# Expert 0 of a routed layer: one list in two passes with the same weights, in place of two lists

## The chip, the cores and the metric

The kernel runs on one core of one Trainium2 chip. A core has five engines, each with an instruction stream of its own that it works through in order: TensorE (PE: matrix products, with weight loading PEld beside them), VectorE (DVE), ScalarE (ACT), GpSimd (POOL) and SyncE (SP), which here only issues transfers. Transfers run on 16 DMA engines. The metric is the device time of one execution in microseconds. The kernel before takes 766.38 us, the median of three runs (764.54, 766.38 and 768.68).

## The reference

Three layers, in float32. Attention with 8 heads of 64 over two sequences of 768 tokens, with a window of 128 and 4 sink tokens, gives x of 1536 x 512. A dense layer follows: h = x w_in, g = h - tanh(h), x = g w_out, with 2048 hidden units. The last layer is routed over 8 experts with 1024 hidden units each:

```
logits = x @ w_gate
noisy  = logits + log1p(exp(x @ w_noise)) * noise
top2   = the two largest of noisy, per token;  top2_w = softmax over the two
for e in range(8):
    for k in range(2):
        mask = top2[:, k] == e
        out[mask] += top2_w[mask, k, None] * (relu(x[mask] @ w1[e]) @ w2[e])
```

So each token goes through two of the experts, and which ones is known only when its row of the dense layer's output is there.

## The kernel before

**Split products.** Products are made in fp32r, TensorE's reduced float32. To keep the accuracy, both operands are split in two parts of that type, `hi` and `lo`: ScalarE casts `hi` (L231 for weights, L967 for rows), VectorE subtracts to get `lo` (L232, L969). Each product then is three: hi hi, lo hi, hi lo.

**Order of the work.** Tokens are 12 blocks of 128; two blocks are a chunk, and there are six chunks. The first 96 units (`N1`) are attention and the dense layer. The last two chunks are the late ones: their dense units come last. After a chunk's dense output its route is computed (`route`, a generator whose steps are called between the units of other work): logits, exp and log, the two largest, the token's position in the lists of its experts. GpSimd then scatters the token's row, with its weights and target row, into two lists in DRAM (`xs`).

**The routed layer.** A list is gathered from DRAM to SBUF as `xr` by four transfers that SP issues (`b_gather`, L909), turned by four VectorE transposes into `xf` (L949) and split into `xg`. `b_tab` fetches the table of weights and target rows, and `settle` (L936 to L939) makes the scale from it. Expert e then has eight units of 128 hidden columns, two per pair d of weights. A unit is `b_l1` (12 products into `h`, L984), `b_chain` (ScalarE relu L994, VectorE L995, which together give `hh`) and `b_l2` (12 products into the four accumulators `yacc`, L1008). At an expert's end `b_evac` copies the accumulators to `yt` (L1022), two by ScalarE and two by VectorE; during the next expert's first four units `b_out` turns them back (L1050), scales them and adds what was gathered of the output before (`prev`, by `b_prev`), and GpSimd stores the rows (L1036).

**Weights.** A pair's weights (1 MB) are loaded into `rawi<d>` by `load_d` (L187), in two buffers, and split into `wi<d>` and `wo<d>`, four buffers of each. A load is issued when the split two pairs earlier has freed its buffer; `emit` works on these splits step by step. Expert 0 has pairs 8 to 11, expert 1 has 12 to 15, and so on.

**Expert 0 in two lists.** While expert 0 runs, the late chunks are still being routed. Its list has 296 places and only rows of the early chunks. The late chunks' rows for expert 0 go to a ninth list of 160 places, which runs after expert 7 with weights loaded once more, in plain fp32 without a split (`c_rows`, `c_l1` L1066, `c_l2` L1078). All other lists have 424 places. Expert 1 begins when the late rows are scattered and gathered; the last route runs between expert 0's first units. Rows beyond a list's places are done by `beyond`, which is not entered with these inputs.

**What sets the order.** From unit N1 - 1 to N1 + 9 every engine's order is that of the code (`in_order`). Outside of that a scheduler places each engine's instructions by its own estimates, and each engine then takes them in that fixed order: one that waits holds up all behind it.

Of the kernel before, what the change touches and what calls it, by code (L numbers as in the profile page):

```python
# [16 lines left out]
P = 128  # L17
# [3 lines left out]
SLOTS_A = 296  # L21
SLOTS_B = 160
FAR = 1 << 20
EARLY_D = 12
# [47 lines left out]
def kernel(ctx: ExitStack, tc: tile.TileContext, qkv, vsink, w64, wm, wgn, noise, out,  # L72
# [14 lines left out]
    WB = SLOTS_B  # L87
# [4 lines left out]
    OT = (max(NT - W, LATE * CT - WA, NT - LATE * CT - WB) + P - 1) // P  # L92
    SEC = NT + P
    ROWS = (E + 1) * SEC
# [6 lines left out]
    N = N1 + E * NU2  # L101
# [71 lines left out]
    def load_d(kind, d, q=nc.sync):  # L173
        if kind == "c" and d >= 2:
            t = gp2.tile([P, 2048], F32, tag="wi", name=f"raw{kind}{d}", bufs=2)
        elif d != EARLY_D:
            t = wp.tile([P, 2048], F32, tag="raw", name=f"raw{kind}{d}", bufs=2)
        if d < 8 and kind != "c":
            q.dma_start(t.bitcast(I32), w64[d * 2 + (kind == "o")].bitcast(I32))
            raw[kind, d] = t  # L180
        elif kind == "c":
            q.dma_start(t, wm[d])
            raw["c", d] = t
        else:
            if d == EARLY_D:
                t = yp.tile([P, 4, 512], F32, tag="y", name=f"raw{kind}{d}", bufs=1).rearrange("p a n -> p (a n)")
# [492 lines left out]
    def route(c0, c1):  # L679
# [7 lines left out]
        tr = {}  # L687

# [44 lines left out]
        pos, ev, zz = [sm[:, i:i + 2] for i in range(2, 8, 2)]  # L733
# [36 lines left out]
        if c0 == LATE:  # L770
            V.tensor_copy(macc[:, T1], macc[:, T0])
            V.memset(macc[:, T1, 0:1], 0.0)
# [14 lines left out]
        if end:  # L787
            V.tensor_scalar(zz, ev, 0.0, float(E), op0=ALU.is_equal, op1=ALU.mult)
            V.tensor_add(ev, ev, zz)
# [4 lines left out]
        V.tensor_scalar(rs, dd, 1.0, 1e-9, op0=ALU.add, op1=ALU.add)  # L794
        V.reciprocal(rs, rs)
        for c in range(c0, c1):
            x, ms = x2s[c], slice((c - c0) * CB, (c - c0 + 1) * CB)
            xi = x.bitcast(I32)
            V.tensor_copy(x[:, :, 516], ev[:, 0, ms])
            V.tensor_copy(xi[:, :, 517], sl[:, 0, ms])  # L800
            V.tensor_copy(x[:, :, 514], rs[:, ms])
            V.tensor_mul(x[:, :, 515], dd[:, ms], rs[:, ms])
# [22 lines left out]
    def overflow_tiles():  # L825

        cnt = cst.tile([P, E + 1], F32, name="cnt")
        caps = cst.tile([P, E + 1], F32, name="caps")
        over = cst.tile([P, E + 1, OT], F32, name="over")
        full = cst.tile([P, E + 2], F32, name="full")  # L830
        nt = cst.tile([P, E + 2], I32, name="nt")
        nc.gpsimd.memset(caps, float(W))
        nc.gpsimd.memset(caps[:, 0:1], float(WA))
        nc.gpsimd.memset(caps[:, E:], float(WB))
        nc.vector.tensor_copy(cnt[:, 0:1], macc[:, LATE * CB, 0:1])
        nc.vector.tensor_copy(cnt[:, 1:E], macc[:, NBLK + 1, 1:])
# [18 lines left out]
    def width(v):  # L855
        return WA if v == 0 else WB if v == E else W

    def tiles(v):
        w = width(v)
        return [(m, o, min(P, w - o)) for m, o in enumerate(range(0, w, P))]  # L860
# [3 lines left out]
    def clear(v):  # L864
# [3 lines left out]
        if v <= E:  # L868
            n = (width(v) + P - 1) // P
# [5 lines left out]
        else:  # L875
            o = (v - E - 1) * NT // 3
# [20 lines left out]
    def b_gather(v):  # L897
        w = width(v)

        xr[v] = []  # L900
        ins = []
        for h, (g0, g1) in enumerate(parts(v)):
            if v:
                r = yp.tile([P, WP // 32, 4, 32], F32, tag="xr", name=f"xr{v}", bufs=1)
            else:
                r = wp.tile([P, 8, 4, 32], F32, tag="cacz"[2 * h:2 * h + 2], name=f"xr{v}_{h}", bufs=1)
            src = xs[v * SEC + 32 * g0:v * SEC + 32 * g1, :512].rearrange("(g t) (q c) -> q t g c", t=32, q=4)
            for q in range(4):
                ins.append(nc.sync.dma_start(r[32 * q:32 * q + 32, :g1 - g0].rearrange("t g k j -> t g (k j)"), src[q]))  # L909
            xr[v].append(r)  # L910
        behind(v, ins, scat)
        if v:
            b_tab(v)

    def behind(v, ins, scatters):

        for i in ins:
            for j in scatters:
                if v or j not in late:
                    wait_for(i, j)  # L920
                else:
                    tc.declare_no_dep(i.ins, j.ins, reason="different rows")
# [515 lines left out]
```

## Time and profile before

| | us |
|---|---|
| median of three runs | 766.38 |
| the profiled run | 767.55 |
| its span | 765.2 |
| TensorE busy in it | 722.1 |
| VectorE busy in it | 473.8 |
| ScalarE busy in it | 356.2 |
| GpSimd busy in it | 185.5 |

The span goes from the first instruction to the last; the profiled run's time is 2.35 us longer. Busy time tells which engine can set the time over all; where it does, and what it waits for, stands in the views by place, which are shown below as rows. A row of a timeline is a run of like instructions: start, length, engine and line, operation, output from input, tile and shape, count, and in brackets the idle time just before with what ended it. Lengths of rows overlap, because products are pipelined: the time of a group is read from its start to the next one's.

### The profile page before, as it was taken

Reading aid. Unit: us, or ns where it says so; the run is one execution under the profiler, and the core shown is the slowest. Engines: PE = TensorE matmul, PEld = TensorE weight load, DVE = VectorE, ACT = ScalarE, POOL = GpSimd, SP = SyncE. Lnnn points to the kernel's source line nnn. Section 1 sums busy time; section 2 is a strip of 40 time slices with the busy share of each in tenths; the row PEclk is TensorE's granted clock in tenths of the full one; section 3 lists DMA queues with packets and bytes.
Section 4 is the critical chain, followed back from the end, with each engine's and each line's share of the span. In section 5 each row is a group of like instructions: output and inputs, shape, how many; then the busy total and the mean of one; then the engine's idle time right before and its main releaser. Section 6 shows DMA issues by size and latency. Waiting matters only on the chain. (4 is left out here: it accounts for less than half of the span.)

```text
span 765.2 us, 12079 instructions
## 1 busy us (share of the span) xinstructions
PE 722.1 (94%) x4346; PEld 652.2 (85%) x4346; DVE 473.8 (62%) x1203; ACT 356.2 (47%) x785; POOL 185.5 (24%) x217
## 2 busy tenths in 40 slices
PE   6888889999999999999999979999999999999991
PEld 3575768888999999988888979999999999999991
DVE  5897658877877486437468666676656474543221
ACT  4877658775644344235446534444343434332110
POOL 5435436531000000000352221313131313132321
PEclk9999989999999999999999989999999999999997
DMA  8988851001432032000235387856657444444411
GB/s 297 247 244 232 213 200 49 24 1 56 166 110 93 18 116 105 1 1 1 84 132 193 125 219 217 238 158 193 190 184 184 165 156 154 151 144 162 155 73 35
DMA packets 64453, 104.96 MB, mean 137 GB/s; under 512 B 19661, under 2 KB 48973, under 8 KB 57728
## 3 DMA queue, kind: packets, MB, share of 16 engines
q1 hardware_dynamic: 57648, 83.35, 36.4%
q0 software_dynamic: 6592, 19.70, 7.6%
q10 hardware_dynamic: 144, 1.05, 0.3%
q8 instruction: 36, 0.59, 0.3%
q14 instruction: 33, 0.27, 0.1%
HBM read 79.12 MB, written 25.68 MB: 137 GB/s over the span
## 5 line engine op out<-in xcount | busy, mean ns | idle before, releaser
L984 PE MATMUL h<-xg,wi 128*128 128x424 f32 (+1 forms) x768 | 158.4, 356 | 4.2 <-ACT xg L967 4.2
L606 PE MATMUL h<-xT,wi 128*128 128x256 f32 x1152 | 157.6, 283 | 1.2 <-DVE th L616 1.2
L606 PEld LDWEIGHTS h<-xT,wi 128*128 128x128 f32 x1152 | 150.4, 189 | 8.2 <-DVE th L616 1.6
L1008 PE MATMUL y<-hh,wo 128*128 128x424 f32 (+1 forms) x768 | 152.1, 348 | 0.2 <-DVE yt L1022 0.2
L638 PE MATMUL acc<-wo,g 128*128 128x512 f32 x576 | 151.6, 397 | 0.0
L984 PEld LDWEIGHTS h<-xg,wi 128*128 128x128 f32 x768 | 139.7, 191 | 8.6 <-ACT xg L967 5.2
L1008 PEld LDWEIGHTS y<-hh,wo 128*128 128x128 f32 x768 | 139.5, 188 | 3.5 <-DVE yt L1022 0.8
L638 PEld LDWEIGHTS acc<-wo,g 128*128 128x128 f32 x576 | 101.9, 190 | 16.3
L994 ACT ACTIVATE hh<-h 128x424 fp32r<-128x424 f32 (+1 forms) x64 | 32.6, 511 | 150.7 <-PE h L984 148.1
L1036 POOL DMA_INDIRECT out<-y,tab x33 | 41.4, 1255 | 191.2 <-DVE y L1035 190.9
L805 POOL DMA_INDIRECT xs<-x,sl x24 | 27.1, 1130 | 236.5 <-PE acc L638 200.9
L995 DVE SCALAR_TENSOR_TENSOR hh<-h,hh 128x424 fp32r<-128x424 f32 (+1 forms) x64 | 37.1, 579 | 75.2 <-ACT hh L994 74.9
L406 POOL TENSOR_TENSOR e<-e,nm 128x528 f32<-128x528 f32 (+1 forms) x48 | 50.6, 1054 | 89.1 <-DVE nm L404 48.9
L619 ACT CAST g<-th 128x256 fp32r<-128x256 f32 x96 | 38.8, 405 | 57.0 <-PE acc L638 40.3
L614 ACT ACTIVATE th<-h 128x256 f32<-128x256 f32 x96 | 36.6, 381 | 59.6 <-PE h L606 57.7
L616 DVE TENSOR_TENSOR th<-h,th 128x256 f32<-128x256 f32 x96 | 40.3, 420 | 38.3 <-ACT th L614 37.9
L395 ACT ACTIVATE e<-e,nm 128x264 f32<-128x264 f32 (+1 forms) x96 | 47.1, 492 | 31.6 <-DVE nm L382 30.8
L621 DVE TENSOR_TENSOR g<-th,g 128x256 fp32r<-128x256 f32 x96 | 41.7, 435 | 23.2 <-ACT g L619 22.5
L486 PE MATMUL xb<-pT,v 128*128 128x256 f32 x220 | 49.0, 351 | 5.3 <-DVE xT L501 5.0
L232 DVE TENSOR_TENSOR wi<-rawi,wi 128x1024 fp32r<-128x1024 f32 x32 | 39.0, 1222 | 20.5 <-ACT wi L231 20.5
L486 PEld LDWEIGHTS xb<-pT,v 128*128 128x128 f32 x220 | 33.3, 196 | 15.6 <-issue 6.2
L889 POOL DMA_INDIRECT prev<-out,tab x33 | 35.7, 1082 | 43.2 <-DMA out<-y,tab 31.3
(170 smaller groups left out, 886.8 us busy)
## 6 DMA issues: line engine op xcount, KB each, us to landing
rawi<-wm SPq DMA_DIRECT2D x31, 1024.0 KB, 5.2
rawi<-w SPq DMA_DIRECT2D x8, 1024.0 KB, 4.8
rawo<-w SPq DMA_DIRECT2D x8, 1024.0 KB, 4.8
xs<-zero SPq DMA_DIRECT2D x7, 1040.0 KB, 7.3
xr<-xs SPq DMA_DIRECT2D x28, 224.0 KB, 6.4
qr<-qkv SPq DMA_DIRECT2D x23, 256.0 KB, 3.1
rawc<-wm SPq DMA_DIRECT2D x4, 1024.0 KB, 5.3
out<-zero SPq DMA_DIRECT2D x3, 1024.0 KB, 7.6
```

The source lines that it names most:

```text
L232: nc.vector.tensor_sub(t[:, 1], r, t[:, 0].bitcast(F32))
L395: nc.scalar.activation(e[:, h], e[:, h], AF.Exp, bias=nm[:, h, 0:1], scale=-1.0, accum_out=nm[:, h, 2:3])
L406: nc.gpsimd.tensor_mul(e, e, nm[:, :, 3:4].to_broadcast([P, 2, C]))
L486: nc.tensor.matmul(o, l, r_, start=t == 0, stop=t == len(todo) - 1)
L606: nc.tensor.matmul(h[:, :CT], w[:, wa, k * 256 + s * P:k * 256 + (s + 1) * P], x[:, k, xa, ts], start=t == 0, stop=t == 11)
L616: nc.vector.tensor_sub(th, h[:, :CT], th)
L619: nc.scalar.copy(g[:, 0], th)
L621: nc.vector.tensor_sub(g[:, 1], th, g[:, 0].bitcast(F32))
L638: i = nc.tensor.matmul(acc[c][m], g[:, ga, m * P:(m + 1) * P], w[:, wa, s:s + 512], start=first and t == 0, stop=done and t == 2)
L984: nc.tensor.matmul(h[:, :width(e)], w[:, wa, k * 256 + s * P:k * 256 + (s + 1) * P], xg[e][:, k, xa, :width(e)], start=t == 0, stop=t == 11)
L1008: nc.tensor.matmul(yacc[e][m][:, :width(e)], w[:, wa, s + m * P:s + (m + 1) * P], g[:, ga], start=u == 0 and t == 0, stop=u == NU2 - 1 and ...
L1036: i = nc.gpsimd.indirect_dma_start(out=out[:, :], out_offset=bass.IndirectOffsetOnAxis(ap=t[:n, m, 1:2], axis=0), in_=y, in_offset=None, b ...
```

## The change

Expert 0 becomes one list of 424 places that is computed in two passes over the same split weights `wi8` to `wi11` and `wo8` to `wo11`. Pass 0 takes rows 0 to 255, pass 1 rows 256 to 423. The early chunks fill the list from its start; the late chunks' rows begin at row 256, or behind the early ones where there are more than 256 (`macc` at `T1`). Pass 0's units are N1 to N1 + 7, pass 1's N1 + 8 to N1 + 15 (104 to 111 by number of unit: `hh104` to `hh111`, since N1 is 96); expert 1 begins with unit 112. Both passes add into the same accumulators, in different columns, and are emptied together after pass 1.

The ninth list, its functions and its weight loads go. So does the early load of pair 12 into another buffer; loads from pair 12 on are held until pass 1's gather is issued. The table of ScalarE's functions for the last route is loaded ahead (`preload_act_table_set`), and the steps of that route are placed anew between the first units. The order is fixed to one unit more at the front (from N1 - 2). `beyond` becomes a loop over the experts.

```diff
-SLOTS_A = 296
-SLOTS_B = 160
+SLOTS_A = 256
...
-    ROWS = (E + 1) * SEC
+    ROWS = E * SEC
+    passes = [(0, 0, WA), (0, WA, W)] + [(e, 0, W) for e in range(1, E)]
...
-    N = N1 + E * NU2
+    N = N1 + (E + 1) * NU2
...
+        if c0 == LATE:
+
+            nc.tensor.matmul(lp[:, 511:512], ones, macc[:, T0, 0:1], start=True, stop=True)
+            nc.vector.tensor_copy(macc[:, T1], macc[:, T0])
+            nc.vector.tensor_scalar(macc[:, T1, 0:1], lp[:, 511:512], float(WA), 1.0 / P, op0=ALU.max, op1=ALU.mult)
...
-    def b_gather(v):
-        w = width(v)
+    def b_gather(i):
+        e, lo, hi = passes[i]
...
-                nc.tensor.matmul(h[:, :width(e)], w[:, wa, k * 256 + s * P:k * 256 + (s + 1) * P],
-                                 xg[e][:, k, xa, :width(e)], start=t == 0, stop=t == 11)
+                nc.tensor.matmul(h[:, :hi - lo], w[:, wa, k * 256 + s * P:k * 256 + (s + 1) * P],
+                                 xg[e][:, k, xa, lo:hi], start=t == 0, stop=t == 11)
...
-                nc.tensor.matmul(yacc[e][m][:, :width(e)], w[:, wa, s + m * P:s + (m + 1) * P], g[:, ga],
+                nc.tensor.matmul(yacc[e][m][:, lo:hi], w[:, wa, s + m * P:s + (m + 1) * P], g[:, ga],
...
-            if hold[0] and todo_load[-1] in (("i", 14), ("i", 15)):
+            if hold[0] and todo_load[-1][1] >= 12:
...
+        if n == N1 - 1:
+            nc.scalar.preload_act_table_set("natural_log_exp_and_others")
...
     b_l1(N1, lambda: r(2))
+    b_l1(N1 + 1, lambda: r(2), 4)
     b_chain(N1)
-    b_l1(N1 + 1, lambda: r(2))
+    r(1)
     for n in range(N1, N):
         marks["a", n] = mark()
-        e, u, d = b_at(n)
+        i, u = divmod(n - N1, NU2)
+        e, d = passes[i][0], b_at(n)[2]
         if n == N1:
-            r(2)
-        if n == N1 + 1:
             r(1)
-        edge = e == 0 and u >= NU2 - 2
-        if n + 1 < N and not (edge and u == NU2 - 1):
+        edge = i == 0 and u >= NU2 - 2
+        if n + 1 < N and n != N1 and not (edge and u == NU2 - 1):
             b_chain(n + 1)
         if n + 2 < N and not edge:
             need("i", b_at(n + 2)[2])
             b_l1(n + 2)
-        if n == N1 + 1:
+        if n == N1:
             r(1)
-        if n >= N1 + 3 and n != N1 + 7:
+        if N1 < n < N1 + 3 or i:
             emit(1, min(d + 3, ND - 1))
         need("o", d)
         b_l2(n)
-        if n == N1 + 1:
+        if n == N1:
+            r(1)
+            b_chain(n + 1)
             r(2)
-        if n == N1 + 2:
-            emit(2, 11)
+            emit(1, 11)
+            b_gather(1)
+            hold[0] = False
+            while held:
+                load_d(*held.pop(0))
             b_tab(0)
-        if e == 0 and u == 4:
+        if i == 0 and u == 4:
             nt = overflow_tiles()
-        if e and u < 4:
+        if i > 1 and u < 4:
             b_out(e - 1, u)
-        if u == 4 and e:
+        if u == 4 and i:
             b_prev(e)
-        if u == NU2 - 1:
+        if u == NU2 - 1 and i:
             b_evac(e)
-        if e + 1 < E:
-            if u == (4 if e == 0 else 1):
-                b_gather(e + 1)
-            if u == (7 if e == 0 else 4):
-                b_trans(e + 1, range(4))
-            if edge and u == NU2 - 1:
-                hold[0] = False
-                while held:
-                    load_d(*held.pop(0), q=nc.scalar)
-                b_prev(0)
-                b_l1(n + 1)
-                b_chain(n + 1)
-                b_l1(n + 2)
-        elif u == 5:
-            c_rows()
-        elif u == 6:
-            load_next()
-            load_next()
-    c_l1(0)
-    for u in range(NU2):
-        if u + 1 < NU2:
-            c_l1(u + 1)
-        c_l2(u)
-        if u < 4:
-            b_out(E - 1, u)
-        if u == 4:
-            b_prev(E)
-    b_evac(E)
+        if e + 1 < E and i:
+            if u == (0 if i == 1 else 1):
+                b_gather(i + 1)
+                b_tab(e + 1)
+            if u == 4:
+                b_trans(i + 1, range(4))
+        if edge and u == NU2 - 1:
+            b_trans(1, range(4))
+            b_l1(n + 1)
+            b_chain(n + 1)
+            b_l1(n + 2)
     for m in range(4):
-        b_out(E, m)
+        b_out(E - 1, m)
     T = mybir.EngineType
-    in_order(marks["a", N1 - 1], marks["a", N1 + 10], (T.PE, T.DVE, T.Activation, T.Pool, T.SP))
+    in_order(marks["a", N1 - 2], marks["a", N1 + 10], (T.PE, T.DVE, T.Activation, T.Pool, T.SP))
```

Two places show what now stands where. The first is VectorE's order from the units before expert 1's first (`hh` is a unit's hidden activations, `xf` turned rows, `xg` their split, `wi`/`wo` split weights). Before, from expert 1's first unit on, whose number was 104:

```order
L995 SCALAR_TENSOR_TENSOR hh104_5320<-h104_5307,hh104_5320 128x424
L995 SCALAR_TENSOR_TENSOR hh105_5336<-h105_5323,hh105_5336 128x424
L232 TENSOR_TENSOR wi14_5354<-rawi14_5291,wi14_5354 128x1024
L232 TENSOR_TENSOR wi15_5448<-rawi15_5352,wi15_5448 128x1024
L232 TENSOR_TENSOR wo15_5488<-rawi15_5352,wo15_5488 128x1024
L1035 SCALAR_TENSOR_TENSOR y0_5378<-yp0_0_5373,tab0_5111,prev0_5297 128x512
L995 SCALAR_TENSOR_TENSOR hh106_5383<-h106_5339,hh106_5383 128x424
L232 TENSOR_TENSOR wo14_5399<-rawi14_5291,wo14_5399 128x1024
L995 SCALAR_TENSOR_TENSOR hh107_5430<-h107_5386,hh107_5430 128x424
L1035 SCALAR_TENSOR_TENSOR y0_5378<-yp0_1_5414,tab0_5111,prev0_5297 128x512
```

Its `hh` stand among weight splits; the rows of expert 1 were turned ahead of this piece. In the changed kernel, from pass 1's third unit (106) to expert 1's first (112):

```order
L959 SCALAR_TENSOR_TENSOR hh106_5313<-h106_5279,hh106_5313 128x168
L925 STREAM_TRANSPOSE xf2_0_5454<-xr2_5306 128x448
...
L929 TENSOR_TENSOR xg1_5453<-xf2_3_5460,xg1_5453 128x424
...
L959 SCALAR_TENSOR_TENSOR hh107_5341<-h107_5316,hh107_5341 128x168
...
L222 TENSOR_TENSOR wi13_5421<-rawi13_5292,wi13_5421 128x1024
L222 TENSOR_TENSOR wo12_5388<-rawi12_5055,wo12_5388 128x1024
L959 SCALAR_TENSOR_TENSOR hh108_5372<-h108_5344,hh108_5372 128x168
L925 STREAM_TRANSPOSE xf3_0_5797<-xr3_5657 128x448
L959 SCALAR_TENSOR_TENSOR hh109_5403<-h109_5375,hh109_5403 128x168
...
L222 TENSOR_TENSOR wo13_5486<-rawi13_5292,wo13_5486 128x1024
...
L222 TENSOR_TENSOR wi15_5588<-rawi15_5517,wi15_5588 128x1024
...
L959 SCALAR_TENSOR_TENSOR hh112_5534<-h112_5504,hh112_5534 128x424
```

The transposes and splits of the rows of pass 2 and 3 (`xf2`, `xf3`: experts 1 and 2) and the weight splits of pairs 12 to 15 now stand among the `hh` of pass 1.

The second is SP's queue of transfers at the same place: weight loads (`rawi`), row gathers (`xr`) and tables. Before, where expert 2 is gathered:

```order
L187 DMA rawi15_5352<-wm 128x2048
L909 DMA xr2_5423<-xs_63 32x14x128 x4
L930 DMA tab2_5428<-xs_63 128x4x8
L187 DMA rawi16_5446<-wm 128x2048
L187 DMA rawi17_5519<-wm 128x2048
L909 DMA xr3_5757<-xs_63 32x14x128 x2
L187 DMA rawi18_5617<-wm 128x2048
```

In the changed kernel, from the load of pair 12, behind pass 1's own gather, on:

```order
L177 DMA rawi12_5055<-wm 128x2048
L177 DMA rawi13_5292<-wm 128x2048
L883 DMA xr2_5306<-xs_63 32x14x128 x4
...
L883 DMA xr3_5657<-xs_63 32x14x128 x3
L177 DMA rawi14_5419<-wm 128x2048
L883 DMA xr3_5657<-xs_63 32x14x128
L883 DMA xr4_6000<-xs_63 32x14x128
L177 DMA rawi15_5517<-wm 128x2048
L883 DMA xr4_6000<-xs_63 32x14x128 x3
```

Gathers of experts 2 and 3 (`xr3`, `xr4`) now stand between and behind the loads of pairs 14 and 15, and a gather's four transfers are no longer in one piece.

## Rows read from the trace of the kernel before

**Rows 1.** the page: span, then busy time of each engine and its instructions

```profile
span 765.2 us, 12079 instructions
PE 722.1 (94%) x4346; PEld 652.2 (85%) x4346; DVE 473.8 (62%) x1203; ACT 356.2 (47%) x785; POOL 185.5 (24%) x217
```

**Rows 2.** PE waits, 418 to 520 us: engine line, releaser, us, times, longest

```profile
PE h L984 <- ACT xg L967: 4.2, 1, 4.2
PE pp L779 <- DVE rt L769: 0.5, 1, 0.5
```

**Rows 3.** timeline of PE there: start us, us, what, count, idle before

```profile
434.05 1.81 PE L984 MATMUL h<-xg,wi 128*128 128x296 f32 x12
435.70 1.80 PE L1008 MATMUL y<-hh,wo 128*128 128x296 f32 x12
...
455.11 10.12 PE L984 MATMUL h<-xg,wi 128*128 128x424 f32 x36 [4.24 <-ACT xg L967]
465.07 2.49 PE L1008 MATMUL y<-hh,wo 128*128 128x424 f32 x12
467.39 0.60 PE L1050 MATMUL yp<-ident,yt 128*128 128x128 f32 x4
```

**Rows 4.** one window: us, PE, PEld, DVE, ACT, POOL, granted clock, DMA, GB/s

```profile
456.00:458.00 2.00, 2.00 (x6) 1.53 (x6) 2.00 (x6) 0.64 (x2) 0.00 (x0) 0.50 0.38 35
```

**Rows 5.** PE in 300 to 322 us: products with 256 and 512 columns

```profile
304.08 1.58 PE L606 MATMUL h<-xT,wi 128*128 128x256 f32 x12
305.50 1.55 PE L638 MATMUL acc<-wo,g 128*128 128x512 f32 x6
```

**Rows 6.** PE in 418 to 520 us: products with 16 columns

```profile
423.99 1.85 PE L717 MATMUL lp<-wg_sb,x2T 128*128 128x16 f32 x16
425.69 2.43 PE L984 MATMUL h<-xg,wi 128*128 128x296 f32 x16
```

**Rows 7.** PE in 83.5 to 98 us: fp32 products of 132 columns

```profile
89.35 0.55 PE L371 MATMUL s<-kT,qT 64*128 64x132 f32 x6
89.83 1.13 PE L486 MATMUL xb<-pT,v 128*128 128x256 f32 x4
```

**Rows 8.** PE in 655 to 766 us: ninth list

```profile
729.16 2.33 PE L1066 MATMUL hc<-xc,rawc 128*128 128x160 f32 x16
...
743.95 1.25 PE L1078 MATMUL yc<-gc,rawc 128*128 128x160 f32 x8
745.04 1.25 PE L1066 MATMUL hc<-xc,rawc 128*128 128x160 f32 x8
...
748.30 1.15 PE L1050 MATMUL yp<-ident,yt 128*128 128x128 f32 x8
```

**Rows 9.** POOL in 740 to 766 us: its last instruction

```profile
751.62 0.91 POOL L1036 DMA_INDIRECT out<-y,tab  x1 [0.30 <-issue]
```

**Rows 10.** DVE in 428 to 480 us

```profile
447.77 1.22 DVE L232 TENSOR_TENSOR wo<-rawi,wo 128x1024 fp32r<-128x1024 f32 x1
...
453.83 2.23 DVE L949 STREAM_TRANSPOSE xf<-xr 128x448 f32<-128x448 f32 x4 [2.46 <-DMA xr<-xs]
455.98 2.09 DVE L969 TENSOR_TENSOR xg<-xf,xg 128x424 fp32r<-128x424 f32 x4
...
458.61 0.17 DVE L939 TENSOR_TENSOR tab<-tab 128x4 f32<-128x4 f32 x1
```

**Rows 11.** ACT in 440 to 480 us

```profile
446.32 1.05 ACT L231 CAST wo<-rawi 128x1024 fp32r<-128x1024 f32 x1
```

**Rows 12.** SP in 428 to 460 us

```profile
444.07 1.89 SPq L909 DMA_DIRECT2D xr<-xs  x4
```

**Rows 13.** DMA issues of the whole page: KB each, us to landing

```profile
rawi<-wm SPq DMA_DIRECT2D x31, 1024.0 KB, 5.2
xr<-xs SPq DMA_DIRECT2D x28, 224.0 KB, 6.4
```

**Rows 14.** DMA issues in 485.4 to 486.6 us

```profile
xr<-xs SPq DMA_DIRECT2D x2, 224.0 KB, 8.9
```

More of the change, by code (lines that the diff above doesn't have):

```diff
@@ L732, in route @@
         dd, rs = sm[:, 0], sm[:, 1]
-        pos, ev, zz = [sm[:, i:i + 2] for i in range(2, 8, 2)]
+        pos, ev = [sm[:, i:i + 2] for i in range(2, 6, 2)]
         V = nc.vector
@@ L785, in route @@
         yield
-        if end:
-            V.tensor_scalar(zz, ev, 0.0, float(E), op0=ALU.is_equal, op1=ALU.mult)
-            V.tensor_add(ev, ev, zz)
+        info = [(x2s[c], slice((c - c0) * CB, (c - c0 + 1) * CB)) for c in range(c0, c1)]
+        V.tensor_scalar(rs, dd, 1.0, 1e-9, op0=ALU.add, op1=ALU.add)
+        V.reciprocal(rs, rs)
+        for x, ms in info:
+            V.tensor_copy(x[:, :, 516], ev[:, 0, ms])
+            V.tensor_copy(x[:, :, 514], rs[:, ms])
+            V.tensor_mul(x[:, :, 515], dd[:, ms], rs[:, ms])
         V.tensor_tensor(o12, o12, ppv[:, None].to_broadcast([P, 2, nb, E]), ALU.mult)
@@ L793, in route @@
         V.scalar_tensor_tensor(sl, ev, float(SEC), pos, op0=ALU.mult, op1=ALU.add)
[L794 to L802, printed above, removed]
+        for x, ms in info:
+            V.tensor_copy(x.bitcast(I32)[:, :, 517], sl[:, 0, ms])
         def scatter(m, k, behind=None):
@@ L853 @@
     prev = {}
-    def width(v):
-        return WA if v == 0 else WB if v == E else W
-    def tiles(v):
-        w = width(v)
-        return [(m, o, min(P, w - o)) for m, o in enumerate(range(0, w, P))]
+    tiles = [(m, o, min(P, W - o)) for m, o in enumerate(range(0, W, P))]
     zero = cst.tile([P, PITCH // 2], F32, name="zero")
@@ L867, in clear @@
             nc.gpsimd.memset(zero, 0.0)
-        if v <= E:
-            n = (width(v) + P - 1) // P
+        if v < E:
+            n = len(tiles)
             nc.sync.dma_start(xs[v * SEC:v * SEC + n * P].rearrange("(p m) (b d) -> p (m b) d", p=P, b=2),
@@ L895, in wait_for, with behind @@
             mybir.DependencyClass.Sync, mybir.DependencyReason.DATA), reason="rows")
-    def b_gather(v):
-        w = width(v)
-        xr[v] = []
+    def b_gather(i):
+        e, lo, hi = passes[i]
+        n = (hi - lo + 31) // 32
         ins = []
[L902 to L915, printed above, removed]
-        for i in ins:
[L918 to L922, printed above, removed]
-        if v == 0:
-            early.extend(ins)
+        if i > 1:
+            r = yp.tile([P, WP // 32, 4, 32], F32, tag="xr", name=f"xr{i}", bufs=1)
+        else:
+            r = wp.tile([P, 8, 4, 32], F32, tag=("ca", "cz")[i], name=f"xr{i}", bufs=1)
+        src = xs[e * SEC + lo:e * SEC + lo + 32 * n, :512].rearrange("(g t) (q c) -> q t g c", t=32, q=4)
+        for q in range(4):
+            ins.append(nc.sync.dma_start(r[32 * q:32 * q + 32, :n].rearrange("t g k j -> t g (k j)"), src[q]))
+        xr[i] = r
+        behind(ins)
+        if i == 0:
+            early.extend(ins)
+    def behind(ins):
+        for i in ins:
+            for j in scat:
+                wait_for(i, j)
     def b_tab(v):
         t = gp2.tile([P, 4, 8], I32, tag="tab", name=f"tab{v}", bufs=3)
-        full = (width(v) + P - 1) // P
-        src = xs[v * SEC:v * SEC + full * P, 512:].rearrange("(m p) w -> p m w", p=P).bitcast(I32)
-        behind(v, [nc.sync.dma_start(t[:, :full], src)], scat)
+        src = xs[v * SEC:v * SEC + 4 * P, 512:].rearrange("(m p) w -> p m w", p=P).bitcast(I32)
+        behind([nc.sync.dma_start(t, src)])
         tabs[v] = t
@@ L1003, in b_l2 @@
         s = (u % 2) * 512
-        if u == 0:
+        if u == 0 and lo == 0:
             yacc[e] = [bank("as"[m // 2], f"y{e}_{m}") for m in range(4)]
@@ L1012, in b_prev @@
         t = tabs[v]
-        settle(t[:, :(width(v) + P - 1) // P], v)
+        settle(t, float(v))
         r = yp.tile([P, 4, 512], F32, tag="prev", name=f"prev{v}", bufs=1)
-        for m, o, n in tiles(v):
+        for m, o, n in tiles:
             gather(r[:n, m], out, t, m, n)
@@ L1142 @@
     todo_load = [(k, d) for d in range(8) for k in "io"] + [("i", d) for d in range(8, ND)]
-    todo_load += [("c", d) for d in range(4)]
     todo_load.reverse()
```

139 lines of the change are left out of this document (44 added, 95 removed).

## The prediction

> **What bounds the kernel now.** I read the page's busy times first: TensorE is busy for 722.1 of 765.2 us, no other engine for more than 473.8 [rows 1]. So a change is worth what it takes out of TensorE's stream or puts in as a pause. The profiled run took 767.55 us, its span and 2.35 us around it; the median of the three runs, 766.38, is 1.17 less. I make the sum against 767.55 and take off 1.17 at its end.
>
> The second view is TensorE's waits around expert 0, since only that place and the end of the kernel are edited. From 418 to 520 us it pauses twice: 4.24 us for `xg`, the turned rows of expert 1, and 0.5 us for `rt` in the last route [rows 2]. The third is the timeline there, which gives prices: twelve products of 296 columns take 435.70 - 434.05 = 1.65 us, so 137 ns each; twelve of 424 columns 467.39 - 465.07 = 2.32 us, so 193 ns; and 36 of them straight behind the pause 465.07 - 455.11 = 9.96 us where 36 x 0.193 = 6.95 were due [rows 3]. The missing 3.0 us are the clock: in the window from 456 to 458 us it was granted at 0.50, the 1.2 GHz level [rows 4]. The pause cost 4.24 + 3.0 = 7.2 us in all.
>
> **The change, part by part, if no wait is added.** The pause before expert 1's first unit goes, because pass 1 stands there now: -7.2 us. The table preload and the new order of the route should end most of the 0.5 us pause: -0.4.
>
> Pass 0 keeps its 8 units x 24 = 192 products, now of 256 columns. Such products took (305.50 - 304.08) / 12 = 118 ns [rows 5], against 137: 192 x 0.019 = -3.6 us.
>
> Pass 1 is new: 192 products of 168 columns. No row has that width in this form. Products of 16 columns took (425.69 - 423.99) / 16 = 106 ns, hardly less than those of 256 [rows 6], so width hardly counts below 256 and I take 107 ns: +20.5 us. From below, products of 132 columns on a stationary tile of 64 rows took 80 ns [rows 7]: 15.4 us. From above, the ninth list's products of 160 columns in plain fp32 took (745.04 - 743.95) / 8 = 136 ns a record, and as a unit's four products leave eight records there, each takes 272 ns [rows 8]: 52.2 us. The form of pass 1 is that of the 256-column row, so I stay near it.
>
> The Trainium skill (TensorE: Matmul & The Clock Gate, LDWEIGHTS) says that loading a stationary operand takes about its columns / 1.2 ns, 107 ns for 128 columns, and the 106 ns above agree with it. By that rule the change loads every weight of expert 0 twice and cannot bring pass 1 below 20.5 us. The same page (Back-to-back issue gap) gives about 81 ns for a product with 128 columns; by that pass 1 would be near 15.6 us and the sum some 5 us lower.
>
> The ninth list goes. From its first product at 729.16 [rows 8] to the end of the last row store at 751.62 + 0.91 = 752.53 [rows 9] are 23.4 us. What stays of it is expert 7's own end, which lay beside the ninth list until now. In the ninth list's end the last transpose starts at 748.30, and 752.53 is 4.2 us later for two row tiles; expert 7 has four, so I add two stores at 0.91 + 0.30 = 1.2 us and 0.5 for wider copies: 7.1 us. That is 23.4 - 7.1 = -16.3. The 12.7 us from 752.53 to the span's end stay. Expert 0 gets one more tile of four transposes, +0.4.
>
> The sum: -7.2 - 0.4 - 3.6 + 20.5 - 16.3 + 0.4 = -6.6, hence 760.9 in the profiled run's terms.
>
> **What is late next.** VectorE and ScalarE take their instructions in order, and the pieces of VectorE's and SP's order under the change show what now stands among pass 1's short units. I reckon on t0, pass 1's start: list 0 ended at 455.11 - 4.24 = 450.87 [rows 3], less 3.6 and 0.4, is 446.9. A pass-1 unit is 24 x 0.107 = 2.57 us, so TensorE wants `hh107` at t0 + 10.2 = 457.1, and expert 1 could start at 446.9 + 20.5 = 467.4.
>
> Before `hh107` VectorE must turn `xr2`, expert 1's rows, which wait for a gather. In before that gather is issued at 444.07 [rows 12] and the first transpose starts at 453.83 after a wait [rows 10]: 9.8 us. Now two loads of 1 MB stand ahead of it on SP's queue; I put the landing a third of such a load (5.2 us, [rows 13]) later, D = 455.5. It is not before `hh106`, at about 452.4, and not later than a whole load, 459.0.
>
> From D on, by durations of before: four transposes 2.15 us and four subtractions 2.0, then the tables till 458.78 [rows 10], so 4.95 after D, and `hh107` at D + 5.35 = 460.9, 3.8 us late. `wi13` and `wo12` at 1.15 each [rows 10]: D + 7.65. Only this frees the buffer for `rawi14`, and behind that load on SP stands the fourth gather of `xr3`. It is issued at D + 8.1. One gather of 224 KB takes 6.4 us in the median and 8.9 in a place right behind a load [rows 13, 14]; its 1.1 us below are 224/1024 of a load's 5.2. I take 5, the load's, as it follows one: D + 13. `xf3_0` waits for it, and `hh109` behind it comes at D + 14 = 469.5, where TensorE wanted it at t0 + 15.4 = 462.3.
>
> The next link is the same once more. `wi14`, three transposes and `wo13` bring D + 18; that frees `rawi15`, which lands at D + 23.7; `wi15` needs a cast of 1.05 [rows 11] and its subtraction, D + 26.2; four subtractions for `xg2` D + 28.3; `wo14` D + 29.5; `hh112`, expert 1's first, at D + 31.2. `rawi16` waits for `wo14` and lands at D + 34.7; `wi16` is split by D + 36.9 = 492.4, and it stands on both engines ahead of the copies that empty expert 0's accumulators, which expert 1's first output products need. Without waits these would start 36 x 0.193 = 6.95 us after 467.4, at 474.3. The added pauses are 492.4 - 474.3 = +18.1 us. In before this cover was one pause at the edge and units of 4.6 us behind it; the units are now 2.6 us long and do not hide the loads.
>
> Pauses of several microseconds bring the clock down afterwards, as behind the 4.24 us pause [rows 4]. That cost 3.0 us there; part of the slower work lies beside the next wait here, so I take 2, from 0 to 3.4.
>
> Sum: -6.6 + 18.1 + 2 = +13.5, 781.0 in the profiled run's terms, and 779.9 on the median's.
>
> **Rivals.**
> 1. The other side, faster: no transfer is late, and VectorE's own work in pass 1 is what decides. In its order from `xf2` to the copies that empty expert 0 stand twelve transposes and eight subtractions for the rows (three times 2.15, twice 2.0: 10.5), seven weight subtractions of 1.15 (8.1), the tables (0.8), seven `hh` and two copies, each put at the 0.5 of one subtraction of 424 columns (4.5): 23.9 us. From the earliest D, 452.4, that ends at 476.3, 2.0 us behind 474.3, and with no long pause the clock stays: 760.9 + 2.0 - 1.2 = 761.7. It decides if each load and gather needs some 2 us in place of 5 and more. For it: DMA was busy at 0.38 behind the pause [rows 4], so there is room. Against it: `rawi15` and `rawi16` can't start before a split that waits itself, and not one row has a load that fast. Chance 0.17.
> 2. Only the first links bind. The transposes of `xr2` are 4 us late and `hh109` 7, and then the loads catch up because TensorE is late as well: +6 to +8 in place of 20, 766 to 768. It depends on `rawi16` landing within 25 us of D, when one of the two loads goes before its wait. Chance 0.15.
> 3. The rate of plain fp32: products of 168 columns pay as plain fp32 does. Then pass 1 lasts 52.2 us, 31.7 more than I put, which itself hides the waits (t0 + 52.2 is 499.1, behind 492.4): 760.9 + 31.7 - 1.2 = 791.4. The point from which it decides is 200 ns a product, where pass 1 (38.4 us) is as long as the whole chain of waits. For it only the rows of plain fp32; against it the 118 ns at 256 columns. Chance 0.05.
>
> **How the numbers follow.** The forecast has 0.63. Its own range: D from 452.4 to 459.0 gives -3.1 and +3.5, the `xr3` gather from 1.1 to 8.9 us -3.9 and +3.9, clock -2 and +1.4; they do not all fall the same way, so 771 to 789. To hold eight of ten the range has to take in rival 2 and reach towards rival 1: 763 to 789. About 0.5%, 3.8 us, is what a measurement of this kernel can tell from no change: same is 762.6 to 770.2. Rival 1 lies on the edge between faster and same, and the sum without waits may itself be 3 us too high or too low: I give faster all of its 0.17, same most of rival 2, 0.13, slower the rest, 0.70.
>
> **What would show it.** Right: TensorE's waits list 15 to 20 us between pass 1's second unit and expert 1's first output product, put down to `hh` on VectorE and to `xr3`, `rawi15` and `rawi16` behind it; pass 1's own products at 107 ns; no product of 160 columns, and about 7 us from the last output product of expert 7 to the last store. Wrong: pass 1 that runs through in some 21 us (rival 1), pauses that end at `hh109` (rival 2), or products of 168 columns near 272 ns (rival 3).

## The result and the profile after

The changed kernel takes 776.26 us, the median of four runs (773.58 to 776.95), beside 767.53 for the kernel before on the same chip: 1.0111 times as long, with a 95% interval from 1.0082 to 1.0140. That is 8.7 us slower, where 13.5 were forecast; it lies within the range, 3.6 us below the 779.9 put for the median. The profiled run, from which the rows below come, took 773.58 us and is the fastest of the four, so its span is only 6.7 us longer than that of the kernel before.

TensorE's waits from 405 to 525 us (engine and line, releaser, us in total, times, longest) no longer have the pause for `xg` of [rows 2]. In its place (one of the three pauses for `hh`, 0.76 us, lies in pass 0):

```profile
PE h L944 <- DVE hh L959: 9.1, 3, 5.3
PE y L972 <- ACT yt L986: 1.3, 1, 1.3
PE y L972 <- DVE yt L986: 0.5, 1, 0.5
```

Where they stand is seen in TensorE's timeline, the counterpart of [rows 3] (start, length, line and operation, tiles, shape, count, idle time before):

```profile
415.69 1.58 PE L944 MATMUL h<-xg,wi 128*128 128x256 f32 x12
...
443.02 4.14 PE L944 MATMUL h<-xg,wi 128*128 128x168 f32 x36
447.00 1.50 PE L972 MATMUL y<-hh,wo 128*128 128x168 f32 x12
448.34 1.50 PE L944 MATMUL h<-xg,wi 128*128 128x168 f32 x12
...
459.20 2.85 PE L944 MATMUL h<-xg,wi 128*128 128x168 f32 x12 [5.34 <-DVE hh L959]
461.85 2.76 PE L972 MATMUL y<-hh,wo 128*128 128x168 f32 x12
464.41 2.76 PE L944 MATMUL h<-xg,wi 128*128 128x168 f32 x12
...
474.65 3.46 PE L944 MATMUL h<-xg,wi 128*128 128x424 f32 x12
...
486.05 3.90 PE L944 MATMUL h<-xg,wi 128*128 128x424 f32 x12 [2.97 <-DVE hh L959]
491.25 0.84 PE L972 MATMUL y<-hh,wo 128*128 128x424 f32 x3 [1.30 <-ACT yt L986]
492.61 1.98 PE L972 MATMUL y<-hh,wo 128*128 128x424 f32 x9 [0.51 <-DVE yt L986]
494.43 0.60 PE L1012 MATMUL yp<-ident,yt 128*128 128x128 f32 x4
```

Twelve products of 168 columns take 448.34 - 447.00 = 1.34 us at first, 112 ns each, and 464.41 - 461.85 = 2.56 us behind the first pause, 213 ns. The granted clock goes with it. Windows of 2 us (length, busy time of PE, PEld, DVE, ACT and POOL, then granted clock, DMA share, GB/s) have it at 0.50, the 1.2 GHz level, up to 476 us, and from 459.20 to there TensorE did not pause again:

```profile
456.00:458.00 2.00, 0.00 (x0) 0.00 (x0) 2.00 (x5) 2.00 (x5) 0.00 (x0) 0.55 0.20 38
466.00:468.00 2.00, 2.00 (x11) 2.00 (x11) 0.00 (x0) 0.34 (x1) 0.00 (x0) 0.50 0.30 80
474.00:476.00 2.00, 2.00 (x8) 1.93 (x8) 0.00 (x0) 0.00 (x0) 0.00 (x0) 0.50 0.83 247
476.00:478.00 2.00, 2.00 (x10) 1.91 (x10) 0.00 (x0) 0.00 (x0) 0.00 (x0) 0.83 0.99 365
```

VectorE's timeline, the counterpart of [rows 10], shows what held it up. It sits idle 5.49 us for the gather `xr2`, with `hh107` (458.83) behind the transposes, and 6.69 us for the gather `xr3`, with `hh109` (468.99) behind:

```profile
454.15 2.22 DVE L925 STREAM_TRANSPOSE xf<-xr 128x448 f32<-128x448 f32 x4 [5.49 <-DMA xr<-xs]
...
458.83 0.32 DVE L959 SCALAR_TENSOR_TENSOR hh<-h,hh 128x168 fp32r<-128x168 f32 x1
...
468.42 0.65 DVE L925 STREAM_TRANSPOSE xf<-xr 128x448 f32<-128x448 f32 x1 [6.69 <-DMA xr<-xs]
468.99 0.29 DVE L959 SCALAR_TENSOR_TENSOR hh<-h,hh 128x168 fp32r<-128x168 f32 x1
...
480.03 1.23 DVE L222 TENSOR_TENSOR wi<-rawi,wi 128x1024 fp32r<-128x1024 f32 x1 [6.42 <-ACT wi L221]
...
490.81 1.23 DVE L222 TENSOR_TENSOR wi<-rawi,wi 128x1024 fp32r<-128x1024 f32 x1 [3.26 <-ACT wi L221]
491.96 1.10 DVE L986 COPY yt<-y 128x424 f32<-128x424 f32 x2
```

The last rows are `wi15`, `wi16` and the copies behind it. ScalarE casts these weights first, and its timeline says what it waited for:

```profile
478.95 1.05 ACT L221 CAST wi<-rawi 128x1024 fp32r<-128x1024 f32 x1 [6.31 <-DMA rawi<-wm]
489.74 1.04 ACT L221 CAST wi<-rawi 128x1024 fp32r<-128x1024 f32 x1 [6.18 <-DMA rawi<-wm]
```

At the end, the counterparts of [rows 8, 9] are the last output products, the transposes, and GpSimd's last store, in a span of 771.9 us:

```profile
749.87 7.02 PE L972 MATMUL y<-hh,wo 128*128 128x424 f32 x36
756.72 1.29 PE L1012 MATMUL yp<-ident,yt 128*128 128x128 f32 x8
```

```profile
762.88 0.93 POOL L1000 DMA_INDIRECT out<-y,tab  x1 [0.30 <-issue]
```

Cut at the same points, the two spans compare so (us; the points are starts in the timelines, and the last store's end):

| stretch | before | after | after - before |
|---|---|---|---|
| start to expert 0's first product | 420.39 | 415.69 | -4.7 |
| to the end of list 0, or of pass 0 | 30.48 | 27.33 | -3.2 |
| to the first transpose of expert 0's output, pass 1 in it | 16.52 | 51.41 | +34.9 |
| to the end of expert 7's output products | 261.77 | 262.29 | +0.5 |
| to the end of the last row store | 23.37 | 7.09 | -16.3 |
| to the end of the span | 12.67 | 8.09 | -4.6 |

The third stretch would be 30.8 us without pauses and at full clock (192 products at 112 ns, 48 at 193 ns). So 20.6 us of it are lost. That is more than the whole difference of 6.7 us: without the loss the changed span would be 13.9 us shorter than the one before. The experiments ask what loses them, and where the two gains at the ends come from.

### The profile page after: what moved, and what is told of

The parts are those of the page before. It is cut to its first block, busy times and chain, and to the rows that moved or that the text cites. A ratio compares the mean times of both kernels' runs of the same rounds, so it can differ in the third digit from the quotient of the medians.

```text
span 771.9 us, 12154 instructions
## 1 busy us (share of the span) xinstructions
PE 730.1 (95%) x4408; PEld 659.3 (85%) x4409; DVE 473.4 (61%) x1197; ACT 354.2 (46%) x787; POOL 181.3 (23%) x213
## 4 chain that ended last, share of the span: by engine, by line
PE 42%; issue 29%; DMA 13%; POOL 6%; ACT 4%; DVE 3%; SPq 1%; POOLq 0%; ACTq 0%; DVEq 0%
PE h L596 17%; PE acc L628 16%; DMA prev<-out,tab 6%; DMA out<-y,tab 5%; PE xb L476 4%; POOL out L1000 3%; PE s L361 2%; POOL prev L864 2%; PE pt L443 1%; DMA vsr<-vsink 1%; ACT e L385 1%; DMA wg_sb<-wgn 1%; PE x2p L687 1%; DVE e L372 1%; ACT xT L485 1%
## 5 line engine op out<-in xcount | busy, mean ns | idle before, releaser
L944 PE MATMUL h<-xg,wi 128*128 128x424 f32 (+2 forms) x864 | 172.2, 350 | 9.1 <-DVE hh L959 9.1
L972 PE MATMUL y<-hh,wo 128*128 128x424 f32 (+2 forms) x864 | 166.7, 343 | 1.8 <-ACT yt L986 1.3
L944 PEld LDWEIGHTS h<-xg,wi 128*128 128x128 f32 x864 | 152.7, 197 | 13.0 <-DVE hh L959 9.5
L972 PEld LDWEIGHTS y<-hh,wo 128*128 128x128 f32 x864 | 152.9, 194 | 6.5 <-ACT yt L986 1.9
L628 PEld LDWEIGHTS acc<-wo,g 128*128 128x128 f32 x576 | 101.4, 188 | 16.3
L958 ACT ACTIVATE hh<-h 128x424 fp32r<-128x424 f32 (+2 forms) x72 | 34.8, 485 | 162.5 <-PE h L944 155.1
L959 DVE SCALAR_TENSOR_TENSOR hh<-h,hh 128x424 fp32r<-128x424 f32 (+2 forms) x72 | 39.0, 545 | 81.6 <-ACT hh L958 81.6
L611 DVE TENSOR_TENSOR g<-th,g 128x256 fp32r<-128x256 f32 x96 | 41.4, 432 | 23.4 <-ACT g L609 22.7
L221 ACT CAST wi<-rawi 128x1024 fp32r<-128x1024 f32 x32 | 33.4, 1044 | 29.4 <-DMA rawi<-wm 29.4
```

The source lines that it names most:

```text
L611: nc.vector.tensor_sub(g[:, 1], th, g[:, 0].bitcast(F32))
L628: i = nc.tensor.matmul(acc[c][m], g[:, ga, m * P:(m + 1) * P], w[:, wa, s:s + 512], start=first and t == 0, stop=done and t == 2)
L944: nc.tensor.matmul(h[:, :hi - lo], w[:, wa, k * 256 + s * P:k * 256 + (s + 1) * P], xg[e][:, k, xa, lo:hi], start=t == 0, stop=t == 11)
L959: nc.vector.scalar_tensor_tensor(g[:, 1], h[:, :w], 0.0, g[:, 0].bitcast(F32), op0=ALU.max, op1=ALU.subtract)
L972: nc.tensor.matmul(yacc[e][m][:, lo:hi], w[:, wa, s + m * P:s + (m + 1) * P], g[:, ga], start=u == 0 and t == 0, stop=u == NU2 - 1 and t == 2)
```

## The experiments

The theory is that of the prediction: engines that work in order stand at waits for gathers and weights, with `hh` behind them. The first rival is that gathers and weights are late in any order, because pass 1's units are too short.

**The code's own order, to unit N1 + 23.** The edit, on the changed kernel:

```diff
-    in_order(marks["a", N1 - 2], marks["a", N1 + 10], (T.PE, T.DVE, T.Activation, T.Pool, T.SP))
+    in_order(marks["a", N1 - 2], marks["a", N1 + 24], (T.PE, T.DVE, T.Activation, T.Pool, T.SP))
```

> The changed kernel with the code's own order kept on every engine to unit N1 + 23 instead of N1 + 9: VectorE now takes hh107 to hh109 ahead of xf2, and xf3, wi15 and wi16 behind the copies that empty expert 0. Same work, same transfers. Theory (the engines' order makes the pauses): in the trace of the changed kernel 51.4 us lie between pass 1's first product (443.02) and the end of expert 1's first output products (494.43), and 20.6 of them are pauses and the 1.2 GHz stretch behind them; 17 to 20 us come back, 776.3 becomes 756 to 759, and no pause between the two is over 1 us. Rival (weights and rows come too late whatever the order, since each pair of weights serves only 2.7 us units): pauses of 10 us or more stay, put down to rawi or xr, and the time is 766 to 776.

Measured: 753.89 us, 0.9814 of the kernel before (0.9763 to 0.9866), and 755.44 in a second series (0.9861, 0.9807 to 0.9914): 0.6 to 2.1 us below the theory's range. TensorE's timeline shows pass 1 without a pause over 1 us, and a window in the middle of it has the granted clock at 1.00:

```profile
443.90 4.14 PE L944 MATMUL h<-xg,wi 128*128 128x168 f32 x36
...
463.60 2.60 PE L944 MATMUL h<-xg,wi 128*128 128x424 f32 x12 [0.81 <-DVE hh L959]
...
473.36 2.49 PE L972 MATMUL y<-hh,wo 128*128 128x424 f32 x12
475.69 0.60 PE L1012 MATMUL yp<-ident,yt 128*128 128x128 f32 x4
```

```profile
456.00:458.00 2.00, 2.00 (x20) 2.00 (x20) 0.93 (x2) 1.25 (x2) 0.00 (x0) 1.00 0.48 90
```

From 443.90 to 475.69 are 31.8 us where the changed kernel has 51.4: 19.6 of the 20.6 are back. VectorE now takes `hh107` to `hh109` and three weight splits ahead of `xr2`'s transposes, which start at 459.07 and wait for nothing:

```profile
457.41 1.22 DVE L222 TENSOR_TENSOR wi<-rawi,wi 128x1024 fp32r<-128x1024 f32 x1 [0.60 <-ACT wi L221]
...
459.07 2.23 DVE L925 STREAM_TRANSPOSE xf<-xr 128x448 f32<-128x448 f32 x4
```

The rival falls: the same loads and gathers, in another order, serve units of the same length in time. Which engine's order counts for how much this run does not show, since it fixes all five: on SP's queue the gather `xr3`, issued from 456.40 on and ahead of `rawi14` in the changed kernel, now is issued from 469.47 on, behind the loads up to `rawi16`. This version is faster than both kernels.

**The gather of expert 1 first.** `b_gather(2)` moves ahead of the held loads; the scheduler's order of the engines stays free.

```diff
             b_gather(1)
+            b_gather(2)
             hold[0] = False
...
-                b_gather(i + 1)
+                if i > 1:
+                    b_gather(i + 1)
```

> The changed kernel with the gather of expert 1's rows (xr2) issued right behind pass 1's own gather, ahead of the loads of pairs 12 and 13. The engines' order stays the scheduler's. Theory: xr2 lands at about 443 to 445 instead of 454, the 5.3 us pause at hh107 goes and the clock does not fall there, hh109 finds xr3 landed; the last links (wo14 frees rawi16, wi16 stands ahead of the copies of expert 0) still hold up expert 1's first output product by some 8 to 10 us: 764 to 769. Rival (the transfers as a whole are too slow, moving one only delays others): same as the changed kernel within 3 us, 773 to 779.

Measured: 768.41 us (1.0006 of before, 0.9975 to 1.0036), 7.9 less than the changed kernel. The 5.34 us pause is gone, and the last links stay:

```profile
452.21 1.57 PE L944 MATMUL h<-xg,wi 128*128 128x168 f32 x12 [0.18 <-DVE hh L959]
...
467.54 4.00 PE L944 MATMUL h<-xg,wi 128*128 128x424 f32 x12 [1.18 <-DVE hh L959]
...
479.10 2.59 PE L944 MATMUL h<-xg,wi 128*128 128x424 f32 x12 [2.59 <-DVE hh L959]
484.87 4.91 PE L972 MATMUL y<-hh,wo 128*128 128x424 f32 x12 [3.18 <-ACT yt L986]
```

So the start of the chain, moved alone, moves expert 1's first output product from 491.25 to 484.87, and no further. The stretch from pass 1's start to the first transpose is 45.7 us here, 5.7 less than in the changed kernel. One part of the expectation missed: `hh109` did not find `xr3` landed, and a pause of 1.38 us stands there.

**The code's order to unit N1 + 16 only.** As the first edit, with `N1 + 17` in place of `N1 + 24`. VectorE then still has `wi16` between the two copies of expert 0's accumulators.

> The changed kernel with the code's order kept to unit N1 + 16 only. hh107 to hh109 come ahead of xf2 as in the run to N1 + 23, but one copy of expert 0's accumulators still stands behind wi16, which waits for rawi16, which waits for wo14, which stands behind xf3. Theory (that last link binds by itself): no pause to hh111, then one of 4 to 7 us before expert 1's first output product and some clock behind it: 758 to 764. Rival (only the first links, hh107 and hh109, made the loss, and the last was late because they were): 752 to 756, as with the longer order.

Measured: 766.25 us (0.9991 of before, 0.9960 to 1.0022), 2 us more than the theory's upper end and far from the rival's. Up to `hh111` pass 1 has two pauses, of 1.04 and 0.82 us, where none was expected; then the output products of expert 1 wait, at low clock:

```profile
482.54 2.96 PE L972 MATMUL y<-hh,wo 128*128 128x424 f32 x6 [3.33 <-ACT yt L986]
486.51 2.78 PE L972 MATMUL y<-hh,wo 128*128 128x424 f32 x6 [1.01 <-ACT yt L986]
```

The last links bind by themselves, but not only the one that was named. The first and longer of these two pauses ends with ScalarE's copy at 481.98. It stands behind the casts of expert 2's rows, those behind VectorE's transposes, and these wait for the `xr3` gather itself. Only the second pause is that of `rawi16` and `wi16` (rows of VectorE and ScalarE):

```profile
478.14 0.65 DVE L925 STREAM_TRANSPOSE xf<-xr 128x448 f32<-128x448 f32 x1 [5.06 <-DMA xr<-xs]
...
478.82 0.55 ACT L927 CAST xg<-xf 128x424 fp32r<-128x424 f32 x1 [5.44 <-DVE xf L925]
...
485.00 1.04 ACT L221 CAST wi<-rawi 128x1024 fp32r<-128x1024 f32 x1 [2.52 <-DMA rawi<-wm]
485.95 0.51 ACT L986 COPY yt<-y 128x424 f32<-128x424 f32 x1
```

In this trace the stretch from pass 1's start to the first transpose is 40.8 us, 9.0 more than in the longer order.

**The same fix on the kernel before.** Its `in_order` ends at N1 + 16, the end of expert 1 there, instead of N1 + 10.

> The kernel before, its code order kept on every engine to the end of expert 1 (unit N1 + 15) instead of unit N1 + 9: the same fix as in the run with the changed kernel's order kept to the end of expert 1. Theory (that fix is worth what the engines' order makes late, and here only the 4.24 us pause for expert 1's rows stands, which a transfer makes): 764 to 769, no difference. Rival (the scheduler's order costs some 20 us in the kernel before as well, and the two passes are no gain in themselves): 748 to 758.

Measured: 765.66 us, 0.9999 of the kernel before (0.9964 to 1.0035). Its one pause at the edge, 3.2 us for `xg`, stays. So the fix shows no gain without the change, and with it 21 to 22 us: with its order mended, the change is a gain of 10 to 12 us (753.89 and 755.44 beside 765.66, in three series whose kernels before lie within 1.1 us of each other).

**The code's order to the end.** `in_order` ends with the last instruction.

> The changed kernel with the code's order kept on every engine to the end. Theory (the scheduler's order costs only where units are short and buffers are about to change hands, at the edge to expert 1; later experts' pauses were 0.7 us in all): 752 to 757, as with the order kept to N1 + 23. Rival (the code's order has gathers and weight splits late for the later experts): 760 or more, with pauses at each expert's start.

Measured: 755.75 us (0.9857 of before, 0.9814 to 0.9900), the same as to N1 + 23. No loss to order shows in the later experts.

**Attention as before.** The first part of the table, -4.7 us, stands where nothing was edited but the zeroing of lists. This kernel zeroes three tiles of 128 rows of list 0 at first, as before (768 half rows, which the expectation counts), and the rest later:

```diff
-            n = len(tiles)
+            n = 3 if v == 0 else len(tiles)
```

> The changed kernel with the first list's zeroing of 1024 rows made 768 rows as it was before, and the 128 rows that the gathers still need zeroed in a later transfer. This gives TensorE's stream of attention the order that it had before. The trace of the changed kernel reaches expert 0's first product 4.7 us earlier (415.69 against 420.39), and most of that is there by 130 us. Theory (the scheduler placed the attention differently because the first zeroing is larger, and that order has no 3.8 us pause at 102.7): the gain is lost again, 779 to 782, first product of expert 0 at about 420. Rival (that pause is chance, and differs between runs): 774 to 778, no difference.

Measured: 775.82 us, as the changed kernel; expert 0's first product is at 416.31. The theory falls. TensorE's attention has the order of the kernel before again, and it pauses all the same, 3.39 us for `xT`, one group of products earlier than the 3.79 us for `pT` before. Behind both stands the same wait, and its place is all in which VectorE's order up to 200 us differs between the two. VectorE's cast of the gate's weights (`wg_r`) waits for their load, behind the subtractions for `xT` in the kernel before and ahead of them here (VectorE before, then VectorE and TensorE in this run):

```profile
104.74 0.19 DVE L663 CAST wg_r<-wg_sb 128x64 fp32r<-128x64 f32 x1 [4.18 <-DMA wg_sb<-wgn]
```

```profile
100.84 0.20 DVE L653 CAST wg_r<-wg_sb 128x64 fp32r<-128x64 f32 x1 [3.27 <-DMA wg_sb<-wgn]
...
102.21 0.76 PE L476 MATMUL xb<-pT,v 128*128 128x256 f32 x3 [3.39 <-DVE xT L491]
```

The rival falls as well, since the pause is no chance: two more traces with the attention code of the kernel before have it for `pT` (3.94 us in the run with the same fix on it, 3.98 in the last run below), and all those of the changed kernel's attention have one for `xT` (1.0 to 3.0 us). How much of the 4.7 us is real remains open: the first product of expert 0 came at 417.58 to 420.39 in the three traces with the attention code of the kernel before, and at 413.74 to 420.98 in nine with that of the changed kernel.

**The end of the program.** The last part of the table, -4.6 us, stands behind the last store, where `beyond` is skipped. On the changed kernel, with its eight bodies written out:

```diff
-            with tc.For_i(0, E, 1) as e:
-                n = nc.values_load(nt[0:1, bass.ds(e, 1)], min_val=0, max_val=OT)
+            for e in range(E):
+                n = nc.values_load(nt[0:1, e:e + 1], min_val=0, max_val=OT)
```

> The changed kernel with the code beyond the widths, which is not entered, written out for the eight experts as before instead of one loop over them. From the end of the last row store to the span's end the kernel before has 12.67 us and the changed one 8.1. Theory (the length of the code that is skipped at the end sets this, by some 0.55 us an expert): about 12 us at the end again, 779 to 782. Rival (it is the store's own landing and the program's end, whatever the code): 8 us, 775 to 778.

Measured: 777.92 us (1.0137 of before, 1.0085 to 1.0189); behind the last store are 12.43 us. The trace has the theory's size. The median is only 1.7 us above the changed kernel's and lies in the rival's range, so the times do not tell the two apart. On the kernel with the order kept to N1 + 23 the question was put again:

> The changed kernel with the code's order kept to unit N1 + 23, once more, beside the three runs that differ from it at the end of the program. 751 to 757.

> The same with the code beyond the widths, which is not entered, written out for eight experts. Theory (it lengthens what follows the last row store from 8.1 to 12.4 us, and that is paid in full): 4 us slower than the run beside it, 756 to 760. Rival (the time before the last store varies more than this, or part of it lies outside the span anyway): within 2 us of it.

Measured: 755.44 and 759.84 us, with 8.10 and 12.87 us behind the last store: 4.8 us in the traces, of which the medians show 4.4. Their intervals (0.9807 to 0.9914, and 0.9880 to 0.9947 of before) overlap, but the other two versions of this series with a short end, at 755.75 and 756.27 us, bear the difference out.

> The same without the code beyond the widths, which is left out together with the question whether it is needed. Theory (that question and the jump over its code are what follows the last store): 4 to 7 us behind the last store in place of 8.1, and 1 to 4 us faster, 750 to 753. Rival (the last store's own landing sets those 8 us): no difference.

Measured: 756.27 us with 8.06 us behind the last store. The remaining 8 us are not the jump's. They are not the store's landing either, which was the rival's reason: it landed 2.2 us after its issue, 1.3 us behind its own end. And on the kernel before, with three bodies in place of nine:

> The kernel before, with the code beyond the widths, which is not entered, as one loop over experts 1 to 7 beside list 0 and the ninth list: three bodies where there were nine. Theory (the tail behind the last row store follows the length of that code: 12.67 us with nine bodies, 12.43 with eight, 8.1 with one): 8 to 10 us there and 763 to 766 in place of 767.6. Rival (the tail differs but is hidden by the run's own time around the span): 767 to 768. The trace also shows a second execution of the same attention code: the pause of 3.8 us at 102.7 is there again, if the order makes it, or not, if it was chance.

Measured: 765.4 us (1.0002 of before, 0.9972 to 1.0033) with 11.76 us behind the last store. A line through the lengths fails: nine bodies 12.67, eight 12.43, three 11.76, one 8.09, none 8.06.

The instructions at the `if` around `beyond` show what the step between three and one is made of (engine's queue, instruction, count, its length in ns, start). First the changed kernel, where the last store ends at 763.81, then this run, where it ends at 748.93:

```profile
L1304 PEldq COMPARE_BRANCH  x1: 358/358/358, 760.0 to 760.0; - x1
...
L1304 POOLq INC_SWDGE_SEM  x1: 1950/1950/1950, 761.8 to 761.8; - x1
...
L1357 POOLq DRAIN  x3: 46/113/7252, 763.8 to 771.6; - x3
```

```profile
L1385 PEldq COMPARE_BRANCH  x1: 3322/3322/3322, 745.9 to 745.9; - x1
...
L1385 POOLq INC_SWDGE_SEM  x1: 1988/1988/1988, 750.4 to 750.4; - x1
```

With one body TensorE's queue is past its branch in 0.36 us, and GpSimd's 1.95 us of semaphore work begin ahead of the last store. With three, eight or nine bodies the branch takes 3.3 to 4.1 us, and that work begins 1.5 to 2.8 us behind the last store's end. The last long instruction in every trace is a drain on GpSimd. It takes 7.25 to 7.41 us and follows that work, or the last store where the work began earlier; without the code it starts ahead of the last store and also ends 7.25 us behind it. It makes up most of the 8 us. So the jump costs a step and not a price per body. What makes the branch long is not shown: the queues marked `instruction` moved 1 packet in the changed kernel from 755 us to the end and 8 in the first version with eight bodies, so fetching code would fit.

## Why the prediction was right, and where it was not

**The chain of late engines: right, nearly link by link.** D was put at 455.5 and is 454.15. From D, `hh107` was to end at +5.35 and does at +5.0 (458.83 + 0.32); `hh109` +14, measured +15.1; `wi15` +26.2, measured +27.1; `wi16` 492.4 (D + 36.9), measured 492.04 (+37.9); the output products of expert 1 from 492.4, measured 492.61 for nine of the first twelve. The loss is 20.6 us against 18.1 + 2. The run with the code's order shows that the order makes it, and the two that mend one end of the chain each show that both ends bind. In D there is luck: it was reckoned from a gather issued at 444.07 that lands 11.4 us later. SP issued it from 438.40 on, and the first transpose came 15.75 us after that:

```profile
438.40 6.80 SPq L883 DMA_DIRECT2D xr<-xs  x4
```

**The split of that loss: wrong.** I put 18.1 us as pauses and 2 as clock. The pauses are 5.34 + 2.97 + 1.30 + 0.51 = 10.1; the other 10.5 are slow products. From 459.20 to 474.65 alone, 72 products at 213 ns in place of 112 cost 7.3 us. The error came from taking the length of the low clock from the stretch of [rows 3, 4], where it was over by about 461 us:

```profile
460.00:462.00 2.00, 2.00 (x10) 1.91 (x10) 0.60 (x1) 0.52 (x1) 0.00 (x0) 0.77 1.03 304
```

Slow products ran while the chain was late anyway: the wait at `hh109` lies under them and shows as no pause. So the 2 us of clock, which were to come on top of the chain, were not there as such. That 20.6 still lies near 20.1 is luck in part: pass 1 began 3.9 us earlier than put, the chain's end came only 0.4 earlier, and the wait between them grew.

**t0: wrong by 3.9 us** (443.02 for 446.9), as the part before expert 0 was 4.7 us shorter in this trace. The landing came only 1.35 us earlier, so pass 1's lateness at `hh107` grew from 3.8 to 5.3.

**Pass 0 and pass 1.** 192 products of 256 columns at 118 ns: right (1.42 us for twelve). The wait for `rt` went, but a 0.76 us wait for `hh97` took its place, so the stretch gained 3.2 and not 4.0. Pass 1 at full clock has 112 ns a product, not 107: 0.9 us more. The low bounds, 80 and 81 ns, are excluded and so is 272. About 107 ns is what the Trainium skill (TensorE: Matmul & The Clock Gate, LDWEIGHTS) gives for loading 128 columns. That no product can be faster was the prediction's own reading of it, which the 112 ns here do not contradict. The 81 ns of that page's Back-to-back issue gap, given for 128 columns, do not agree with this row.

**The ninth list:** 23.4 us became 7.09; 7.1 were worked out.

**The step that failed** is "The 12.7 us from 752.53 to the span's end stay." They became 8.1. I had the loop over `beyond` in the change and gave it no cost or gain at all, because it is not entered. The pair of runs on the longer order shows 4.4 us for it. Had it been counted, the sum without waits would be 756.5 on the profiled run, and the forecast 775.5 on the median, 0.8 below the measured one. That nearness is luck in part as well. On the profiled runs the forecast is 7.4 us too high, 773.58 for 781.0: 4.6 us lie behind the last store and 4.7 ahead of expert 0, where nothing was forecast, 0.7 outside the span, and the parts between came out 2.5 us longer than the sum had them.

Of the rivals, the first (transfers in time) fails on the trace, the second (only the first links) on the run to N1 + 16, and the third on the 112 ns.

## What to carry to other kernels

Where a phase of short units is put between two long ones, read for each engine what its fixed order places between the short units' own steps, and follow the waits there from link to link; a gain in work is kept only if those steps go first. Mend the whole chain at once: each end alone gave 8 to 10 of 21 to 22 us. And price what stands at a program's end, code that is jumped over included.

## What the runs showed of the hardware

Behind pauses of like length, 4.24 and 5.34 us, the clock was low for about 6 us with products of 424 columns (from 455.11 to about 461 in the kernel before) and for 17 us with products of 168 (459.20 to 476), where TensorE was busy all the time. In the changed kernel it came back only when products of 424 columns ran again, from 474.65 on; the run with the attention as before repeats this (0.50 from 459.51 to 476 us). With the code's order and no pause over 1 us the same 168-column products ran at 1.00 throughout, so there they did not lower the clock.

The time behind the last store grew from 8.1 to 12.4 and 12.9 us when code that is jumped over was written out eight times, and it was no shorter without that code. TensorE's branch over it took 0.36 us with one body and 3.3 to 4.1 with three or more; a drain on GpSimd behind it took 7.25 to 7.41 us.
